# Paired numerators as two sets of 128 columns, a later share of one output projection, and a reordered last stretch

## The chip, the cores and the metric

The kernel runs on one core of one Trainium2 chip. The metric is the device time in microseconds (us) of one execution; smaller is better.

## What is computed

The input x is 2048 tokens of 512 numbers, all in float32. Two branches are mixed by a gate, token by token:

```
g = sigmoid((x * gate_w).sum(-1))
out = g * A(x) + (1 - g) * B(x)

A:  q, k, v = heads(x @ wqkv)                     # 32 heads of 16
    phi(p) = concat(softmax(p @ w_phi), softmax(-(p @ w_phi)))
    kv = sum over tokens of phi(k)^T v,  z = sum over tokens of phi(k)
    num = phi(q) kv,  den = phi(q) z + 1e-6
    A = concat over heads(num / den) @ wo
B:  per token and head the best of 16 keys in each of two halves: one of 256 experts
    B = sum over heads of gelu(x . u[expert]) * v[expert]
```

## The kernel before

The 2048 tokens are 16 tiles of 128. A first part (up to about 130 us) builds the weights and sums the keys and values of all tiles into `kvb`. The part that the change touches is the second: tile by tile it makes the output. Matrix products in full precision are made of three products of a high part (`xh`, `ch`, written by ScalarE, ACT) and a low part (`xl`, `cl`, the rest, written by VectorE, DVE, or GpSimd, POOL).

What one tile passes through, by the names in the trace:

- `s` (two halves of the scores against the keys), `pq` (the projected queries) and `pp` (the products with the experts' rows and the gate): matrix products, lines 55 to 57, into banks of a ring of four named "mm". DVE reads `s` in `best` (lines 736 and 737) and `pq` in `soft_in` (lines 123 to 129).
- The weighted feature map `d` of the queries. ACT splits it into two planes of 16-bit halves (`pl`, line 757), a DMA on SP's queue transposes them (`tp`, line 759), and ACT joins the halves again into `ptb` (`join`, two calls of `join_half`, line 768). The join of tile t writes the place t % 2 of `ptb`.
- The numerators `oT` = `kvb` times `ptb` (`mid_num`, line 777): 16 small matmuls of 64 rows by 32 columns of weights, 8 heads' worth in two tiles of PSUM. For a pair of tiles the same 16 matmuls take 256 columns, 128 of each tile. ACT turns `oT` into `xh` (`num_hi`, line 785), DVE into `xl` (`num_lo`, line 791).
- The experts' counts (`count`, lines 810 to 842, on DVE), multiplied by the activations into the coefficients `cf` (`coef`, line 846). They are transposed in one of two ways. The long way: ACT splits (`plc`, line 851), SP's queue transposes by DMA (`tpc`, line 853), ACT joins (`ctj`, line 858) and takes the high part (`ch`, line 862), POOL or DVE the low part (`cl`, line 879). The short way, `back_c`: TensorE transposes into `CT` (line 871), ACT takes `ch` (line 874), DVE `cl` (line 879).
- The output projection `po` (called `end` for the last tile): 18 matmuls of 512 columns, in this order: eight that read `xh` (line 891), four that read `xl` (line 891), and six that read `ch` and `cl` (line 898). `store` copies `po` to `ot` on ACT (line 929) and issues a DMA on SP's queue (line 930).

The order of the work on every engine is written out by hand; each engine takes its instructions in that order. The function `turned(a)` holds the order of one turn: it works at the front of tile a+1, in the middle of tile a, and at the back of tiles before it. `mid_num` is called for one tile at a time up to turn 5, then for a pair in the turns 7, 9, 11 and 13; the fifth pair (12 and 13) is in the last stretch. How many of the `po` matmuls are issued by the end of turn a, counted over all tiles, is `due(a)`: 15, 29 and 43 for the turns 2, 3 and 4. `back_some` issues what is due, at two places of a turn, and never past the end of a tile of 18 in one call; when a tile's 18 are out it calls `store`.

After turn 14 comes the last stretch, also written by hand, with a = 15, b = 14 and z = 13: it holds what is left of the tiles 10 to 15.

Of the kernel before, what the change touches and what calls it, by code (L numbers as in the profile page):

```python
# [20 lines left out]
P = 128  # L21
# [13 lines left out]
def mix_kernel(ctx, tc, xT, wqT, wkT, wv, wphi, wo, wq, kk, ug, ev, cst, out):  # L35
    nc = tc.nc
    pe, dve, act, pool, sp = nc.tensor, nc.vector, nc.scalar, nc.gpsimd, nc.sync
# [4 lines left out]
    def mm_bank(name):  # L42
        return psum.tile([P, 512], F32, tag="mm", bufs=4, name=name)

    def tr_bank(name):
        return psum.tile([P, 512], F32, tag="tr", bufs=3, name=name)
# [12 lines left out]
    kvb = per.tile([P, 8, 32], F32, name="kvb")  # L59
# [14 lines left out]
    def x_of(t):  # L74
        first = max(f for f in SEC if f <= t)
        return tuple(xt[i, first][:, t - first] for i in range(2))
# [253 lines left out]
    st8 = {t: {} for t in range(NT)}  # L330
# [146 lines left out]
    for t in range(5, NT - 1, 2):  # L477
        n = t + 1
# [13 lines left out]
        a = pks[t] = mm_bank(f"pk{t}")  # L492
        prod(a, tile_of(t, 0), b11, True)
        b = mm_bank(f"pu{t}")
# [89 lines left out]
    t = NT - 1  # L584
# [41 lines left out]
    def drain(t):  # L626
        while t in chains:
            step(t)
# [30 lines left out]
    def gelu_in(t):  # L659
        px, x2 = st8[t]["G"], st8[t]["x2"]  # L660
        pool.tensor_tensor(x2, x2, px, op=ALU.mult)

    def gelu_act(t):
        x2, gs = st8[t]["x2"], st8[t]["g"]
        act.activation(gs[:, 3:4], gs[:, 2:3], AF.Copy, scale=-0.5, bias=0.5)
        act.activation(x2, x2, AF.Tanh)
        act.activation(x2, x2, AF.Identity, bias=gs[:, 3:4], scale=gs[:, 3:4])

    def gelu_out(t):
        px, x2 = st8[t]["G"], st8[t]["x2"]  # L670
        pool.tensor_tensor(px, x2, px, op=ALU.mult)
# [33 lines left out]
    def soft_y(t, i):  # L705
        e = st8[t]
        dve.tensor_reduce(pair(e["st"][:, 224:288])[:, :, i], hs(e["w"], i), axis=AX.X, op=ALU.add)  # L707
# [45 lines left out]
    def planes(t, i):  # L753
        e = st8[t]
        e.setdefault("tp", [])
        pl = w3.tile([P, 2, 512], U16, tag="pl", name=f"pl{i}_{t}")
        act.copy(pl, e["ph"][:, halves[i]].bitcast(U16).rearrange("p (c j) -> p j c", j=2))  # L757
        tp = w3.tile([P, 8, P], U16, tag="tp", name=f"tp{i}_{t}")
        sp.dma_start_transpose(tp, pl.rearrange("p j c -> p (j c)"))
        e["tp"].append(tp)  # L760

    def join(t):
        for i in range(2):
            join_half(t, i)

    def join_half(t, i):
        p16 = ptb.rearrange("p g t n -> p (g t n)").bitcast(U16).rearrange("p (g t n j) -> p t j g n", j=2, n=P, t=2)
        act.copy(p16[:, t % 2, :, 4 * i:4 * i + 4, :], st8[t]["tp"][i].rearrange("p (j g) n -> p j g n", j=2))  # L768

    def mid_num(*ts):  # L770
        o = [tr_bank(f"oT{q}_{ts[0]}") for q in range(2)]
        u = slice(0, 2) if len(ts) > 1 else slice(ts[0] % 2, ts[0] % 2 + 1)
        n = 2 * P if len(ts) > 1 else P
        for g in range(8):
            for q in range(2):
                r0, c0 = 64 * q, 32 * (g % 4)
                pe.matmul(o[q][c0:c0 + 32, (g // 4) * n:(g // 4 + 1) * n], kvb[r0:r0 + 64, g, :],  # L777
                          ptb[r0:r0 + 64, g, u, :], start=(g < 4), stop=True, skip_group_check=True)
        for i, t in enumerate(ts):
            st8[t]["o"] = x_of(t) + ([m[:, :2 * n].rearrange("p (k t n) -> p t k n", k=2, n=P)[:, i] for m in o],)  # L780

    def num_hi(t):
        oh, ol, o = st8[t]["o"]
        for q in range(2):
            act.copy(oh[:, 2 * q:2 * q + 2], o[q])
# [58 lines left out]
    def coef(t):  # L844
        e = st8[t]
        (pool if t < NT - 1 else dve).tensor_tensor(e["C"], e["C"], e["G"], op=ALU.mult)  # L846

    def c_planes(t):
        e = st8[t]
        pl = w4.tile([P, 2, NX], U16, tag="plc", bufs=1, name=f"plc{t}")  # L850
        act.copy(pl, e["C"].bitcast(U16).rearrange("p (c j) -> p j c", j=2))
        e["tc"] = w4.tile([P, 4, P], U16, tag="tpc", bufs=1, name=f"tpc{t}")
        sp.dma_start_transpose(e["tc"], pl.rearrange("p j c -> p (j c)"))
# [13 lines left out]
    def back_c(t):  # L867
        e = st8[t]
        o = mm_bank(f"CT{t}")
        for j in range(2):  # L870
            pe.transpose(o[:, j * P:(j + 1) * P], e["C"][:, j * P:(j + 1) * P], ident)
        ch = w4.tile([P, 2 * P], F32R, tag="ch", name=f"ch{t}")
        cl = w4.tile([P, 2 * P], F32R, tag="cl", name=f"cl{t}")
        act.copy(ch, o[:, :2 * P])
        e["c"] = (ch, cl, o)

    def back_cl(t, eng=dve):
        ch, cl, o = st8[t]["c"]
        eng.tensor_tensor(cl, o[:, :2 * P], ch, op=ALU.subtract)
# [4 lines left out]
    def back_mm(t, cols=slice(0, D), bank=None):  # L884
        e = st8[t]
        oh, ol, _ = e["o"]
        po = bank
        mms = [(oh[:, k, :], w[k][:, cols]) for k in range(NK) for w in (woh, wol)]
        mms += [(ol[:, k, :], woh[k][:, cols]) for k in range(NK)]
        for i, (a, b) in enumerate(mms):  # L890
            pe.matmul(po, a, b, start=(i == 0), stop=False)  # L891
            yield
        ch, cl, _ = e["c"]
        js = (slice(0, P), slice(P, 2 * P))
        mms = [(ch[:, js[j]], w[:, j, cols]) for j in range(2) for w in (eh, el)]
        mms += [(cl[:, js[j]], eh[:, j, cols]) for j in range(2)]
        for i, (a, b) in enumerate(mms):
            pe.matmul(po, a, b, start=False, stop=(i == 5))  # L898
            yield
# [3 lines left out]
    def back(t, n=18):  # L903
        if t not in backs:
            split_ = t < NT - 5
            e = st8[t]
            e["po"] = psum.tile([P, 512], F32, tag="acc", name=f"po{t}") if split_ else mm_bank(f"po{t}")
            backs[t] = back_mm(t, bank=e["po"])
        for _ in range(n):
            next(backs[t])  # L910
# [1 line left out]
    ran = 0  # L912

    def due(a):
        return 14 * a - (13 if a < 7 else 14)

    def back_some(n):
        nonlocal ran
# [7 lines left out]
    def store(t):  # L926
        po = st8.pop(t)["po"]
        ot = w3.tile([P, D], F32, tag="ot", name=f"ot{t}")
        act.copy(ot, po)
        sp.dma_start(out[t * P:(t + 1) * P, :], ot)  # L930
# [65 lines left out]
    def turned(a):  # L996
# [7 lines left out]
        if a == 2:  # L1004
            mid_num(z)
            num_hi(z)
            gelu_pre(a)
# [6 lines left out]
        if 2 < a < 5:  # L1014
            back_some(due(a) - ran)
# [6 lines left out]
        if a < 5:  # L1022
            if a == 2:
                front_s(n, 1)
            else:
                mid_num(z)
                num_hi(z)
            if a == 3:
                front_s(n, 1)
            if masks:  # L1030
                mid_mask(*masks)
            if a > 3:
                front_s(n, 1)
            soft_exp(a)
        else:
            front_s(n, 1)
            soft_exp(a)
            if nums:
                mid_num(*nums)
            if parted is not None:  # L1040
                num_hi(parted)
            if masks:
                mid_mask(*masks)
            back_some(due(a) - ran)
# [12 lines left out]
        if a == NT - 2:  # L1057
            front_q(n)
        front_p(n, False)
        back_some(due(a) - ran)  # L1060
        best(n, 0)
        soft_y(a, 0)
# [13 lines left out]
    for a in range(NT - 1):  # L1076
        n, b, z = a + 1, a - 1, a - 2
# [4 lines left out]
        if a == 1:  # L1082
# [7 lines left out]
            ptb = spare_[:, :16 * P].rearrange("p (g t n) -> p g t n", t=2, n=P)  # L1090
# [48 lines left out]
    a, b, z = NT - 1, NT - 2, NT - 3  # L1139
# [18 lines left out]
    num_hi(z - 1)  # L1158
    back(z - 2, 6)
    num_hi(z)  # L1160
    join(b)
    store(z - 3)
    soft_y(a, 0)
    soft_y(a, 1)
    for _ in gate(a):
# [3 lines left out]
    coef(z - 1)  # L1169
    coef(z)  # L1170
    c_planes(z - 1)
    planes(a, 0)
    planes(a, 1)
    num_lo(z - 1)
# [10 lines left out]
    c_join(z - 1)  # L1185
    back_cl(z - 1, pool)
    back_c(z)
    store(z - 2)
    gelu_in(a)
    gelu_act(a)  # L1190
    gelu_out(a)
    back(z - 1, 6)
    back(b, 12)
    step(a, 4)
    back_cl(z)
    join(a)
    store(z - 1)
    back(z, 3)
    mid_num(a)
    num_hi(a)  # L1200
    back(z, 3)
    store(z)
    drain(a)
    num_lo(a)
# [1 line left out]
    coef(a)  # L1206
    end = mm_bank("end")
    ends = back_mm(a, bank=end)
    for _ in range(12):
        next(ends)  # L1210
    back_c(b)
    back_c(a)
    back_cl(b)
    back_cl(a)
    back(b, 6)
    store(b)
    for _ in range(6):
# [59 lines left out]
```

## Time and profile before

| | |
|---|---|
| median of 3 runs | 368.77 us (368.05 to 369.68) |
| the profiled execution | 368.4 us |
| its span, first to last instruction | 366.7 us |
| TensorE (PE) busy | 358.5 us, 98% |
| VectorE (DVE) busy | 318.4 us, 87% |
| ScalarE (ACT) busy | 256.7 us, 70% |
| GpSimd (POOL) busy | 207.5 us, 57% |

The profile was taken on one execution; 1.7 us of its 368.4 lie outside the span. "PEld" is TensorE's loading of weights, which runs beside its matmuls. A row of the timeline gives the start, the length, the engine, the line of the kernel, what is written from what, how many instructions are taken together, and in brackets how long the engine was idle before and what ended that. Matmuls overlap: the length of one is over the distance to the next. One of the small float32 matmuls shows as two rows. In the chain of work that ended last, each row is a start, a length and the work that the end waited for at that time.

### The profile page before, as it was taken

To read this page: it belongs to the slowest core of one execution; us is meant where nothing else is said; L and a number is where in the kernel's file an instruction comes from. 1 tells how busy PE (TensorE), PEld (TensorE's weight loads), DVE (VectorE), ACT (ScalarE), POOL (GpSimd) and SP (SyncE) were. 2 spreads that over 40 slices of the span, in tenths; PEclk is the share of its full clock that TensorE was granted. 3 is DMA by queue.
4 is the path that set the end of the run, shared out by engine and by line. 5 is a ranking of instruction groups with operands and counts; after the bars stand their busy time and mean duration, and the time that the engine had idled before them with its cause. 6 is when DMAs were issued, how large, how long until landed. Compare 5 with 4: busy or idle time off the path is not lost.

```text
span 366.7 us, 8308 instructions
## 1 busy us (share of the span) xinstructions
PE 358.5 (98%) x3244; PEld 280.1 (76%) x3244; DVE 318.4 (87%) x639; ACT 256.7 (70%) x455; POOL 207.5 (57%) x205
## 2 busy tenths in 40 slices
PE   8999999999999999999999999999999999999985
PEld 4766767776878878887788887887887887887764
DVE  4679999999878888999998897799879998899781
ACT  5586578876656765795696866866778886765871
POOL 1179989988928847445446546524724736527130
PEclk9999999999999999999999999999999999999999
DMA  7868898558773113144362244234343247234532
GB/s 267 332 241 273 273 259 246 156 179 300 240 212 100 62 30 69 35 86 67 79 116 64 67 86 88 74 86 84 62 98 90 55 104 103 73 88 100 66 93 86
DMA packets 75751, 47.54 MB, mean 130 GB/s; under 512 B 67265, under 2 KB 68161, under 8 KB 73409
## 3 DMA queue, kind: packets, MB, share of 16 engines
q1 hardware_dynamic: 74848, 46.15, 47.9%
q10 hardware_dynamic: 864, 0.87, 0.8%
q8 instruction: 25, 0.41, 0.5%
q14 instruction: 14, 0.11, 0.1%
HBM read 26.43 MB, written 4.19 MB: 84 GB/s over the span
## 4 chain that ended last, share of the span: by engine, by line
PE 75%; DVE 11%; ACT 4%; POOL 4%; DMA 3%; issue 2%; SPq 0%; POOLq 0%; ACTq 0%; DVEq 0%
PE po L891 8%; PE s L55 5%; PE s L57 5%; PE s L56 5%; PE pk L467 5%; PE po L898 4%; PE pu L467 4%; PE ws L300 4%; PE pq L57 3%; PE pq L56 3%; PE pq L55 3%; PE pe L467 2%; PE oT L777 2%; PE kvacc L291 2%; PE pv L467 2%
## 5 line engine op out<-in xcount | busy, mean ns | idle before, releaser
L728 POOL TENSOR_TENSOR d<-d,st 128x512 f32<-128x512 f32 x30 | 32.5, 1105 | 48.2 <-DVE st L721 47.0
L699 POOL TENSOR_TENSOR w<-d,zb 128x512 f32<-128x512 f32 x32 | 41.2, 1310 | 19.8 <-ACT d L693 19.8
L55 PE MATMUL s<-sh,xh 128*128 128x512 f32 x128 | 50.4, 394 | 0.0
L56 PE MATMUL s<-sl,xh 128*128 128x512 f32 x128 | 49.9, 389 | 0.0
L57 PE MATMUL s<-sh,xl 128*128 128x512 f32 x128 | 49.8, 389 | 0.0
L757 ACT COPY pl<-d 128x1024 uint16<-128x1024 uint16 x32 | 33.3, 1047 | 20.2 <-POOL d L728 20.1
L768 ACT COPY ptb<-tp 128x1024 uint16<-128x1024 uint16 x32 | 41.5, 1369 | 0.6 <-DMA tp<-pl 0.4
L284 POOL TENSOR_TENSOR d<-d,st 128x1024 f32<-128x1024 f32 x16 | 32.6, 2036 | 8.7 <-ACT d L275 6.5
L846 POOL TENSOR_TENSOR cf<-cf,px 128x256 f32<-128x256 f32 x15 | 11.1, 741 | 33.5 <-DVE cf L842 33.5
L55 PEld LDWEIGHTS s<-sh,xh 128*128 128x128 f32 x128 | 24.0, 188 | 5.3 <-issue 0.4
L57 PEld LDWEIGHTS s<-sh,xl 128*128 128x128 f32 x128 | 24.0, 188 | 5.0
L56 PEld LDWEIGHTS s<-sl,xh 128*128 128x128 f32 x128 | 24.0, 188 | 4.8
L55 PE MATMUL pq<-wah,xh 128*128 128x512 f32 x64 | 25.2, 393 | 0.0
L57 PE MATMUL pq<-wah,xl 128*128 128x512 f32 x64 | 24.9, 390 | 0.0
L56 PE MATMUL pq<-wal,xh 128*128 128x512 f32 x64 | 24.9, 389 | 0.0
L703 DVE TENSOR_REDUCE st<-d 128x32 f32<-128x512 f32 x32 | 20.5, 678 | 4.3 <-ACT d L693 4.1
L164 DVE TENSOR_TENSOR xl<-xr,xh 128x512 fp32r<-128x512 f32 (+2 forms) x17 | 21.7, 1292 | 1.7 <-ACT xh L160 1.6
L737 DVE TENSOR_TENSOR eq<-s,mx 128x512 bf16<-128x512 f32 x32 | 22.1, 691 | 1.1
L736 DVE TENSOR_REDUCE mx<-s 128x32 f32<-128x512 f32 x32 | 21.7, 680 | 0.2 <-PE s L57 0.2
L707 DVE TENSOR_REDUCE st<-w 128x32 f32<-128x512 f32 x32 | 20.5, 675 | 0.9 <-POOL w L699 0.9
L279 DVE TENSOR_REDUCE st<-d 128x64 f32<-128x1024 f32 x16 | 19.3, 1209 | 2.0 <-ACT d L275 1.9
L275 ACT ACTIVATE d<-d 128x1024 f32<-128x1024 f32 x16 | 17.0, 1066 | 4.1 <-DVE d L129 4.1
(271 smaller groups left out, 1086.2 us busy)
## 6 DMA issues: line engine op xcount, KB each, us to landing
wq<-wq SPq DMA_DIRECT2D x16, 1024.0 KB, 5.5
xr<-xT SPq DMA_DIRECT2D x15, 256.0 KB, 5.3
y<-ot SPq DMA_DIRECT2D x15, 256.0 KB, 2.0
rawk<-wkT SPq DMA_DIRECT2D x1, 1024.0 KB, 5.8
rawq<-wqT SPq DMA_DIRECT2D x1, 1024.0 KB, 6.3
rawu<-ug SPq DMA_DIRECT2D x2, 258.0 KB, 5.9
rawv<-wv ACTq DMA_DIRECT2D x2, 256.0 KB, 4.6
rawv<-wv SPq DMA_DIRECT2D x2, 256.0 KB, 5.3
```

Of the source, the lines that this page charges most:

```text
L55: pe.matmul(o, ah, bh, start=(first and i == 0), stop=False)
L56: pe.matmul(o, ah, bl, start=False, stop=False)
L57: pe.matmul(o, al, bh, start=False, stop=(last and i == n - 1))
L164: dve.tensor_tensor(l[:, ks], rawx[t][:, ks], h[:, ks], op=ALU.subtract)
L284: pool.tensor_tensor(g64(d), g64(d), b64(st[:, 128:192]), op=ALU.mult)
L467: pe.matmul(o, x_, w_, start=(first and i + j == 0), stop=(i == 1 and j == 2), skip_group_check=True)
L699: pool.tensor_tensor(hs(e["w"], i), hs(e["ph"], i), hs(zb, i), op=ALU.mult)
L728: eng.tensor_tensor(g64(d)[:, gs_], g64(d)[:, gs_], r[:, gs_].unsqueeze(2).to_broadcast([P, 32, F]), op=ALU.mult)
L737: dve.tensor_tensor(e["eq"][:, 512 * half:512 * half + 512].rearrange("p (h f) -> p h f", f=F), p3, mx.unsqueeze(2).to_broadcast([P, H, F] ...
L757: act.copy(pl, e["ph"][:, halves[i]].bitcast(U16).rearrange("p (c j) -> p j c", j=2))
L768: act.copy(p16[:, t % 2, :, 4 * i:4 * i + 4, :], st8[t]["tp"][i].rearrange("p (j g) n -> p j g n", j=2))
L891: pe.matmul(po, a, b, start=(i == 0), stop=False)
```

## The change

Four things are changed. (1) `mid_num` for a pair no longer gives each of the 16 weights 256 columns. It goes over the 16 weights with the 128 columns of the first tile, and then again with those of the second: 32 matmuls of 128 columns. The numerators of one tile now lie side by side in PSUM. (2) `due(3)` is 26 in place of 29. (3) In the last stretch the split `plc` of tile 12's coefficients stands between the two halves of the join of tile 14; the stores of the tiles 10, 11 and 12 are later. (4) The last two transposes `back_c` stand after ten of the last tile's matmuls in place of twelve.

```diff
     def mid_num(*ts):
         o = [tr_bank(f"oT{q}_{ts[0]}") for q in range(2)]
-        u = slice(0, 2) if len(ts) > 1 else slice(ts[0] % 2, ts[0] % 2 + 1)
-        n = 2 * P if len(ts) > 1 else P
-        for g in range(8):
-            for q in range(2):
-                r0, c0 = 64 * q, 32 * (g % 4)
-                pe.matmul(o[q][c0:c0 + 32, (g // 4) * n:(g // 4 + 1) * n], kvb[r0:r0 + 64, g, :],
-                          ptb[r0:r0 + 64, g, u, :], start=(g < 4), stop=True, skip_group_check=True)
         for i, t in enumerate(ts):
-            st8[t]["o"] = x_of(t) + ([m[:, :2 * n].rearrange("p (k t n) -> p t k n", k=2, n=P)[:, i] for m in o],)
+            for g in range(8):
+                for q in range(2):
+                    r0, c0 = 64 * q, 32 * (g % 4)
+                    pe.matmul(o[q][c0:c0 + 32, (2 * i + g // 4) * P:(2 * i + g // 4 + 1) * P], kvb[r0:r0 + 64, g, :],
+                              ptb[r0:r0 + 64, g, t % 2, :], start=(i == 0 and g < 4), stop=True, skip_group_check=True)
+            st8[t]["o"] = x_of(t) + ([m[:, 2 * i * P:2 * (i + 1) * P].rearrange("p (k n) -> p k n", n=P) for m in o],)
...
-        return 14 * a - (13 if a < 7 else 14)
+        return 26 if a == 3 else 14 * a - (13 if a < 7 else 14)
...
-    join(b)
-    store(z - 3)
+    join_half(b, 0)
...
     c_planes(z - 1)
+    join_half(b, 1)
     planes(a, 0)
...
-    store(z - 2)
+    store(z - 3)
     gelu_in(a)
     gelu_act(a)
+    store(z - 2)
...
     join(a)
-    store(z - 1)
     back(z, 3)
     mid_num(a)
     num_hi(a)
     back(z, 3)
+    store(z - 1)
     store(z)
...
-    for _ in range(12):
+    for _ in range(10):
         next(ends)
     back_c(b)
     back_c(a)
     back_cl(b)
     back_cl(a)
+    for _ in range(2):
+        next(ends)
     back(b, 6)
```

TensorE between turns 3 and 4, before (`po` is that of tile 1, `pq` that of tile 4):

```order
L891 MATMUL po_2414<-gl,xh_65 128x512
L891 MATMUL po_2414<-wb_77,xh_65 128x512 x2
L891 MATMUL po_2414<-t1h,xl_68 128x512 x2
L891 MATMUL po_2414<-gh,xl_68 128x512
L55 MATMUL pq_2475<-wah,xh_65 128x512
```

The same place in the change:

```order
L889 MATMUL po_2414<-gl,xh_65 128x512
L889 MATMUL po_2414<-wb_77,xh_65 128x512 x2
L55 MATMUL pq_2472<-wah,xh_65 128x512
L56 MATMUL pq_2472<-wal,xh_65 128x512
L57 MATMUL pq_2472<-wah,xl_68 128x512
```

Three matmuls that read `xl` have moved behind the twelve of `pq`.

ScalarE in the last stretch, before, from the join of tile 14 on (`ot_4369` is the store of tile 10, `plc` belongs to tile 12, `pl_15` to tile 15):

```order
L768 COPY ptb<-tp_14_4262 128x2x4x128
L768 COPY ptb<-tp_14_4266 128x2x4x128
L929 COPY ot_4369<-po_4229 128x512
L851 COPY plc_4386<-cf_4376 128x512
L757 COPY pl_15_4390<-d_4285 128x1024
L757 COPY pl_15_4394<-d_4285 128x1024
```

The same place in the change:

```order
L768 COPY ptb<-tp_14_4326 128x2x4x128
L849 COPY plc_4462<-cf_4452 128x512
L768 COPY ptb<-tp_14_4330 128x2x4x128
L757 COPY pl_15_4467<-d_4349 128x1024
L757 COPY pl_15_4471<-d_4349 128x1024
```

The split `plc` has moved ahead of half a join, and the store of tile 10 has left this place.

ScalarE further on, before, up to the join of tile 15 (`ot_4471` is the store of tile 11):

```order
L874 CAST ch_4468<-CT_4465 128x256
L929 COPY ot_4471<-po_4309 128x512
L665 ACTIVATE gs_4296<-gs_4296 128x1
L666 ACTIVATE x_4443<-x_4443 128x256
L667 ACTIVATE x_4443<-x_4443,gs_4296 128x256
L768 COPY ptb<-tp_15_4392 128x2x4x128
```

The same place in the change (`ot_4548` is the store of tile 10, `ot_4555` that of tile 11):

```order
L872 CAST ch_4545<-CT_4542 128x256
L927 COPY ot_4548<-po_4293 128x512
L665 ACTIVATE gs_4360<-gs_4360 128x1
L666 ACTIVATE x_4520<-x_4520 128x256
L667 ACTIVATE x_4520<-x_4520,gs_4360 128x256
L927 COPY ot_4555<-po_4373 128x512
L768 COPY ptb<-tp_15_4469 128x2x4x128
```

The store of tile 10 stands where that of tile 11 stood, and the store of tile 11 directly ahead of the join of tile 15.

## The prediction

> **What bounds the kernel now.** First the page: its first lines give the span and the busy shares.
>
> ```profile
> span 366.7 us, 8308 instructions
> PE 358.5 (98%) x3244; PEld 280.1 (76%) x3244; DVE 318.4 (87%) x639; ACT 256.7 (70%) x455; POOL 207.5 (57%) x205
> ```
>
> TensorE is nearly full, so time is won only by making its work shorter or by taking away one of its few waits. The second view is therefore the list of TensorE's waits over the whole span; these three rows lie in the part that the change touches.
>
> ```profile
> PE po L898 <- ACT ch L862: 1.9, 1, 1.9
> ...
> PE po L891 <- DVE xl L791: 0.3, 1, 0.3
> PE po L898 <- ACT ch L874: 0.2, 1, 0.2
> ```
>
> Each happened once: 1.9, 0.3 and 0.2 us. These 2.4 us are nearly all that the change can win; the rest must come from what TensorE costs to stop and start. The third view is the chain that ended last, read in the last stretch, where the engine that sets the end is no longer TensorE alone.
>
> ```profile
> 340.61 2.47 ACT ptb L768 x2
> 343.08 0.45 ACT ot L929
> 343.53 0.52 ACT plc L851
> ...
> 344.07 4.30 DMA tpc<-plc
> ...
> 348.39 0.77 ACT ctj L858
> ...
> 349.67 0.74 POOL cl L879
> 350.41 1.19 POOL x L661
> ...
> 351.62 0.43 ACT x L666
> ...
> 352.58 2.59 ACT ptb L768 x2
> ...
> 355.21 0.45 PE oT L777 x16
> ...
> 356.56 2.77 PE end L891 x12
> 359.32 0.23 PE CT L871 x2
> ...
> 359.58 0.38 ACT ch L874
> ...
> 360.00 1.66 PE po L898 x6
> ```
>
> The reader is to see that from 340.6 to 355.2 the path runs over ACT, a transposing DMA and POOL, and comes back to TensorE only when the second half of the join of tile 15 is done. What is taken off ACT's row there counts, and what is put on it counts too.
>
> **The pairs as two sets.** A pair's visit now, and a single tile's visit, with the instruction that follows each; then the loads of weights in the single visit.
>
> ```profile
> 338.22 1.09 PE L777 MATMUL oT<-ptb,kvb 64*32 64x256 f32 x32
> 339.25 0.56 PE L800 MATMUL mk<-wm,et 128*128 128x16 bf16 x16
> ...
> 344.85 0.67 PE L777 MATMUL oT<-ptb,kvb 64*32 64x128 f32 x32
> 345.45 0.73 PE L891 MATMUL po<-t1h,xl 128*128 128x512 f32 x2
> ```
>
> ```profile
> 344.85 0.40 PEld L777 LDWEIGHTS oT<-ptb,kvb 64*32 64x32 f32 x32 [0.35 <-issue]
> ```
>
> From first start to the next work a pair takes 1.03 us and a single tile 0.60. The number of matmuls is the same, 16; only the columns double. So 128 columns of all 16 weights cost 0.43, and entering and leaving costs 0.17. Two sets in one visit are 0.17 + 2 × 0.43 = 1.03: no change. The low end is a few hundredths below that; the high end is two whole visits, 1.20, or +0.17 a pair and +0.85 for five. I take zero, since a single visit already reloads its weights at this pace (32 loads in 0.40 of its 0.67). A sentence by itself: the Trainium skill, TensorEngine Tiling, section Performance Considerations (Instruction Overhead), gives each matmul about 60 cycles of overhead; at the 2.4 GHz of its page TensorE: Matmul & The Clock Gate that is an estimate of 25 ns, 0.4 us for 16 more matmuls and 2.0 us for five pairs, which would turn the sum below into a loss of 0.5 us. The row speaks against it: 32 rows in 0.67 us is 21 ns a row with everything in it.
>
> The split does not let ACT begin earlier: in the order with its waits, the conversions `xh` of the pair's first tile carry a wait on TensorE and those of the second carry none, so the first already wait for the last matmul. That is the same as before. ACT and DVE read the same number of columns.
>
> **Three matmuls later in turn 3.** This is where TensorE waited for `xl` of tile 1:
>
> ```profile
> 177.79 0.63 PE L891 MATMUL po<-wb,xh 128*128 128x512 f32 x2
> 178.71 0.74 PE L891 MATMUL po<-t1h,xl 128*128 128x512 f32 x2 [0.30 <-DVE xl L791]
> 179.29 0.39 PE L891 MATMUL po<-gh,xl 128*128 128x512 f32 x1
> ```
>
> Two matmuls take 0.46 when they run without a stop (179.29 − 178.71 = 0.58 here, after the stop). From 177.79 the next should start at 178.25; it started at 178.71. The stop costs 0.46 and the slow start 0.12: 0.58. The change puts the 12 matmuls of `pq` there, whose bank has long been read, and the three come 2.7 us later, when `xl` is done. TensorE is 0.58 ahead from turn 4 on. What is late next? DVE is busy for 13.48 of these 14.00 us (the third engine of the row) and waits for no matmul in them, so it does not come along:
>
> ```profile
> 184.00:198.00 14.00, 14.00 (x97) 11.47 (x97) 13.48 (x33) 10.44 (x20) 6.66 (x8) 1.00 0.48 85
> ```
>
> The nearest thing for which TensorE would then wait is the bank of the second half of `s` of tile 5, which DVE's `best` reads last here, and which the second half of tile 6 needs:
>
> ```profile
> 197.43 0.69 DVE L737 TENSOR_TENSOR eq<-s,mx 128x512 bf16<-128x512 f32 x1
> ```
>
> ```profile
> 198.59 0.39 PE L55 MATMUL s<-sh,xh 128*128 128x512 f32 x1
> ```
>
> DVE is done at 198.12, TensorE would be there at 198.01: a new wait of about 0.16 with a signal's time, and again a slow start of 0.12. I take 0.58 − 0.28 = **0.30** as the gain, between 0 (if it is all given back) and 0.58. From turn 6 on DVE itself waits for `pq`, as here, so the shift is handed on to it:
>
> ```profile
> 237.09 0.69 DVE L123 TENSOR_REDUCE st<-pq 128x32 f32<-128x512 f32 x1 [1.24 <-PE pq L57]
> ```
>
> **The last stretch, up to the 1.9 us wait.** I keep the times of before. `plc` now starts after one half join: 340.61 + 1.24 = 341.85 in place of 343.53. Its input is there: both coefficients of the pair are ready when POOL ends at 341.35.
>
> ```profile
> 339.91 1.44 POOL L846 TENSOR_TENSOR cf<-cf,px 128x256 f32<-128x256 f32 x2 [1.79 <-DVE cf L842]
> ```
>
> The DMA then starts at 342.39 and, at its 4.30, lands at 346.69; the view of this tile gives its landing over all its issues:
>
> ```profile
> DMA to landing us min/median/max: 2.3/2.3/4.3
> ```
>
> So 4.30 is the worst of thirteen, and on SP's queue the store of tile 10 no longer stands ahead of it. ACT's own row, without that store, is 0.45 earlier, and then no longer stops for the DMA:
>
> ```profile
> 348.39 0.76 ACT L858 COPY ctj<-tpc 128x512 uint16<-128x512 uint16 x1 [0.91 <-DMA tpc<-plc]
> ```
>
> ```profile
> 349.64 0.50 PE L898 MATMUL po<-eh,ch 128*128 128x512 f32 x1 [1.86 <-ACT ch L862]
> ```
>
> `ctj` starts at 348.39 − 0.45 − 0.91 = 347.03, after the landing. Everything behind it is 1.36 earlier, the first TensorE matmul on `ch` too: 349.64 becomes 348.28. Of the 1.9 us wait about 0.5 is left, since ACT's row is now the bound. Splitting the join of tile 14 makes its second half 0.07 later (0.52 for `plc`, less 0.45 for the store); TensorE reads it only at 344.85, so that costs nothing.
>
> **From there to the join of tile 15.** POOL's `cl` and `x`, and ACT's two steps behind them, come 1.36 earlier. But the store of tile 11, which ACT did while it waited for POOL, now stands directly ahead of the join: +0.45. The join ends 0.91 earlier. TensorE must wait for it:
>
> ```profile
> 354.64 1.03 PE L777 MATMUL oT<-ptb,kvb 64*32 64x128 f32 x32
> ```
>
> TensorE comes to this visit 5.00 after 349.64 now, hence at 353.28 in the change, is through its first half at 353.73, and the join's second half is there at 355.21 − 0.91 = 354.30. ACT sets the time: **0.91**. Bounds: 1.36 if the store were hidden again; 0.46 if the landing or the join of tile 15 were late by half a microsecond. The store of tile 12, now behind the conversions of tile 15, stands where ACT next waits for the last matmuls of tile 13, and costs nothing.
>
> **The last transposes.**
>
> ```profile
> 359.16 0.60 PE L871 MATMUL CT<-cs,cf 128*128 128x128 f32 x4
> ```
>
> ```profile
> 356.83 0.45 DVE L846 TENSOR_TENSOR cf<-cf,px 128x256 f32<-128x256 f32 x1
> ```
>
> After the four transposes (first row) TensorE waits until 360.00. Two matmuls of 0.23 now fill that: they hide the 0.24 of idle time and some of the transposes' draining, less a slow start. I take **0.30**, between 0.2 and 0.4. The transposes come earlier by 0.91 + 0.46, at 357.8; their last input now ends at 357.28, and DVE's part comes earlier too.
>
> **The sum.** 0 − 0.30 − 0.91 − 0.30 = −1.51 us. Against the profiled execution (span 366.7, 368.4 with what lies around it) that is 366.9. The profiled execution lies 0.4 below the median of the runs, 368.77, so the median becomes 367.3, or −0.41%. About 0.5% (1.84 us) is what a measurement of this kernel can tell from no change.
>
> **The rivals.** *More is hidden* (0.29). Either the wait at 198 does not come, because DVE is a little earlier (+0.28), or ACT's store of tile 11 falls into idle time because a shorter DMA and the earlier TensorE leave some (+0.45). One of them gives −1.8 to −2.0, both −2.2: 366.6 to 367.0, take 366.8. For it: the margin at 198 is 0.1 us. Against: ACT has no idle time left ahead of the join in my account.
>
> *Two sets cost two visits* (0.15). +0.17 a pair, 0.85 in five, four of them in stretches where TensorE never waits, the fifth ahead of ACT's row: −0.7, 368.1. For it: nothing shows 32 such matmuls in one visit. Against: the 0.17 is the change of shape at both ends of a visit.
>
> *The weights are not hidden* (0.06), the slower side. The second set loads the same places of the array that the first is still using. If each load waited for its matmul, a visit would be 0.17 + 0.86 + 2 × 0.40 = 1.83, +0.80 a pair, +4.0 in five: 368.77 − 1.5 + 4.0 = 371.3. It decides from +0.30 a pair on (no gain) and is past 0.5% slower from +0.67. The Trainium skill, TensorE: Matmul & The Clock Gate, Part 3, says that loads overlap matmuls in flight only for another group of rows, and there are only two groups here. Against it: in the single visit weights are changed in the same places halfway, in 0.67 in all.
>
> **How the numbers follow.** The forecast has 0.50, −1.2 to −1.8. Its faster end and the first rival give faster by over 0.5%: 0.05 + 0.29 = 0.34. The rest of the forecast and the second rival lie within 0.5%: 0.45 + 0.15 = 0.60. Slower is the third: 0.06. The range leaves out the third rival and the outer ends of the first two: 366.3 to 368.6.
>
> **What would show it.** In the changed profile: pair visits of 64 rows, 1.05 to 1.12 long, next work 1.03 after the start. No wait for `xl` near 178, and one of 0.1 to 0.3 for `eq` near 198. No wait of ACT for `tpc` in the last stretch; TensorE's wait for `ch` (line 860) 0.4 to 0.7 in place of 1.9; its wait for the join of tile 15 about half a microsecond; no wait for `ch` of line 872 at the end. I am wrong if the pair's visit is over 1.2, if TensorE's wait for `ch` stays above 1 us, or if the gain of turn 3 is gone by the last stretch.

## The result and the profile after

The change runs in 366.94 us (median of 4 runs, 366.46 to 367.27), the kernel before beside it in 369.22 (4 runs, 368.05 to 369.68): a ratio of 0.9942 [0.9914, 0.9971]. Measured a second time, it was 367.15 (8 runs) against 368.86 (15 runs): 0.9933 [0.9905, 0.9961]. So it is faster, by 0.6 to 0.7%: both intervals lie below 1, with their near ends at 0.3% and 0.4%. The forecast was 367.3 and −0.41%: the time lies in the range, the gain is a little larger than foretold. The profiled execution took 367.09 us, with this page:

```profile
span 365.3 us, 8628 instructions
PE 358.8 (98%) x3404; PEld 282.2 (77%) x3404; DVE 318.5 (87%) x639; ACT 256.7 (70%) x455; POOL 206.6 (57%) x205
```

TensorE's share is the same 98%; it has 160 matmul rows and 160 loads more (five pairs of 32), and its busy time is 0.3 longer, not shorter. The gain is in its waits. The list of them, which leaves out stops of about a tenth of a microsecond, now has these:

```profile
PE warm L357 <- POOL tab L339: 1.1, 1, 1.1
PE pv L56 <- DVE wbr L50: 0.6, 1, 0.6
PE pv L55 <- ACT wbr L49: 0.4, 1, 0.4
PE po L896 <- ACT ch L860: 0.3, 1, 0.3
PE oT L776 <- ACT ptb L768: 0.2, 1, 0.2
```

The wait of 1.9 us for `ch` has shrunk to 0.3, those for `xl` and for the last `ch` are gone, and a wait of 0.2 for the join of tile 15 (`ptb`) is there, which the prediction had, only longer. A wait for `eq` near 198, which it also had, is not there. The chain that ended last, in the last stretch:

```profile
343.69 1.85 ACT pl L757 x2
...
347.08 0.69 ACT ctj L856
...
347.80 0.41 ACT ch L860
...
350.67 0.60 ACT x L667
351.28 0.47 ACT ot L927
351.75 2.48 ACT ptb L768 x2
...
354.27 0.45 PE oT L776 x16
```

The transposing DMA, 4.30 us of the chain before, has left it: the path stays on ACT's row up to `ch`, and comes back to it behind POOL's `cl` and `x`. The store of tile 11 (`ot`, 0.47) stands on it now. From 354.27 up to the last copies nothing but TensorE is on the path.

**A measure that can tell tenths.** Full times of single executions swing by one to three microseconds, because the first 150 us do: the first numerators of tile 0 start at 150.95 in the execution before and at 151.40 after, and at 151.45 and 154.04 in the two profiled executions of one kernel (`best`, below). From there on the two profiled executions agree to 0.03, in both kernels that were profiled twice. So the runs below are read by two distances inside the profiled execution. D goes from the start of tile 0's numerators to the start of VectorE's last copy, T from the start of the last pair's numerators to the same copy. The rows of before, then of after, from the timelines of TensorE and VectorE:

```profile
150.95 0.67 PE L777 MATMUL oT<-ptb,kvb 64*32 64x128 f32 x32
```

```profile
363.08 0.42 DVE L1222 COPY ot_end<-end 128x256 f32<-128x256 f32 x1 [2.34 <-PE end L898]
```

```profile
151.40 0.67 PE L776 MATMUL oT<-ptb,kvb 64*32 64x128 f32 x32
...
338.29 1.16 PE L776 MATMUL oT<-ptb,kvb 64*32 64x128 f32 x64
```

```profile
361.68 0.42 DVE L1223 COPY ot_end<-end 128x256 f32<-128x256 f32 x1 [2.33 <-PE end L896]
```

D is 212.13 before and 210.28 after; T is 363.08 − 338.22 = 24.86 before and 23.39 after. So 1.85 us were won, 1.47 of them in the last stretch and 0.38 before it. The second profile of the change gives 210.26 and 23.39; that of `best` 208.99 and 22.63, beside 208.96 and 22.60.

| | D | T | full time of the profiled execution |
|---|---|---|---|
| before | 212.13 | 24.86 | 368.4 |
| the change | 210.28 | 23.39 | 367.09 |
| due_only | 211.18 | 24.83 | 368.82 |
| pairs_one_set | 209.99 | 23.31 | 366.44 |
| sets_of_64 | 212.07 | 23.65 | 369.32 |
| plc_late | 211.36 | 24.47 | 367.53 |
| store10_early | 210.77 | 23.88 | 368.6 |
| store11_hidden | 209.82 | 22.94 | 367.78 |
| end_12 | 210.70 | 23.83 | 367.4 |
| best | 208.96 | 22.60 | 365.73 |
| best_2 | 208.37 | 22.02 | 364.75 |

### The profile page after: what moved, and what is told of

It is laid out like the page before. It is cut to its first block, busy times and chain, and to the rows that moved or that the text cites. A ratio compares the mean times of both kernels' runs of the same rounds, so it can differ in the third digit from the quotient of the medians.

```text
span 365.3 us, 8628 instructions
## 1 busy us (share of the span) xinstructions
PE 358.8 (98%) x3404; PEld 282.2 (77%) x3404; DVE 318.5 (87%) x639; ACT 256.7 (70%) x455; POOL 206.6 (57%) x205
## 4 chain that ended last, share of the span: by engine, by line
PE 86%; ACT 5%; POOL 3%; DMA 2%; DVE 2%; issue 1%; SPq 0%; POOLq 0%; ACTq 0%; DVEq 0%
PE po L889 9%; PE s L55 7%; PE s L56 7%; PE s L57 7%; PE pk L467 5%; PE po L896 5%; PE pu L467 4%; PE ws L300 4%; PE pq L55 4%; PE pq L56 4%; PE pq L57 4%; PE oT L776 2%; PE kvacc L291 2%; PE pp L55 2%; PE pp L56 2%; PE pp L57 2%
## 5 line engine op out<-in xcount | busy, mean ns | idle before, releaser
L927 ACT COPY ot<-po 128x512 f32<-128x512 f32 x15 | 8.7, 589 | 16.3 <-PE po L896 14.8
```

## The experiments

**Only the later share of turn 3 (due_only).** The kernel before, with one line of the change:

```diff
-        return 14 * a - (13 if a < 7 else 14)
+        return 26 if a == 3 else 14 * a - (13 if a < 7 else 14)
```

> The kernel before with due(3) = 26 alone. All distances are taken in one execution from the first numerator matmul of tile 0 (turn 2) to the start of the last copy on VectorE: 212.13 us before, 210.28 in the change. Theory: the stop of TensorE for the low part of tile 1 goes with its slow start, nothing takes its place, and the rest of the loop moves along: 211.5 us, no wait of TensorE near 198 us, and the 1.9 us wait for ch in the last stretch stays, since ScalarE's row moves along too. First rival, as the prediction had it: TensorE then waits for the bank that VectorE's best reads last, 211.8. Second rival: what is won is given back at a later wait, 212.1.

The visit of turn 4 starts 35.69 after tile 0's in the kernel before and 35.10 here: 0.59 won, and in turn 5 (50.45 and 49.86) it is still 0.59. D is 0.95 shorter: 0.59, and 0.33 more that were lost in turn 8 before and not here. The edit alone does not decide these 0.33: the change has it too and lost most of them (last section). T is 24.83 against 24.86, so nothing is given back at the end. TensorE's two waits for `ch`, 1.9 and 0.2, stay, and that for `xl` is gone.

**Pairs as one set in the changed kernel (pairs_one_set).** The change with the numerators of before:

```diff
+        for g in range(8):
+            for q in range(2):
...
+                pe.matmul(o[q][c0:c0 + 32, (g // 4) * n:(g // 4 + 1) * n], kvb[r0:r0 + 64, g, :],
+                          ptb[r0:r0 + 64, g, u, :], start=(g < 4), stop=True, skip_group_check=True)
         for i, t in enumerate(ts):
-            for g in range(8):
-                for q in range(2):
...
-                    pe.matmul(o[q][c0:c0 + 32, (2 * i + g // 4) * P:(2 * i + g // 4 + 1) * P], kvb[r0:r0 + 64, g, :],
-                              ptb[r0:r0 + 64, g, t % 2, :], start=(i == 0 and g < 4), stop=True, skip_group_check=True)
```

> The change with the pair's numerators again as one set of 256 columns; all else as in the change. Theory: the two sets cost 0.06 us in each of five visits, so the distance from the first numerator matmul of tile 0 to the last copy goes from 210.28 to about 209.95 us, and the next work stands 1.03 us after a visit's start in place of 1.09. Rival: the two sets gain something elsewhere (a conversion that starts earlier, reads that lie side by side), then the distance is 210.3 or more.

D is 0.29 shorter than the change's, T 0.08: about 0.07 for each of four pairs. The first pair, in turn 7, shows nothing in D: both kernels start turn 9's visit 104.02 after tile 0's, since the stop in turn 8 is 0.06 longer here (last section). The visits of the last pair show what one costs; first what follows the change's (which starts at 338.29, above), then this run:

```profile
339.38 0.56 PE L798 MATMUL mk<-wm,et 128*128 128x16 bf16 x16
```

```profile
337.81 1.09 PE L777 MATMUL oT<-ptb,kvb 64*32 64x256 f32 x32
338.84 0.31 PE L800 MATMUL mk<-wm,et 128*128 128x16 bf16 x6
```

So two sets take 1.09 to the next work (339.38 − 338.29) and one set 1.03 (338.84 − 337.81). This part of the change loses.

**Pairs as four sets of 64 columns (sets_of_64).** What sets the pace of many small matmuls:

```diff
+            for h in range(2 if len(ts) > 1 else 1):
+                w_ = P // 2 if len(ts) > 1 else P
...
+                        s0 = (2 * i + g // 4) * P + h * w_
+                        pe.matmul(o[q][c0:c0 + 32, s0:s0 + w_], kvb[r0:r0 + 64, g, :],
+                                  ptb[r0:r0 + 64, g, t % 2, h * w_:(h + 1) * w_],
+                                  start=(i == 0 and h == 0 and g < 4), stop=True, skip_group_check=True)
```

> The change with a pair's numerators as four sets of 64 columns (64 matmuls a visit; the same columns and the same result). Theory: the first 16 matmuls of a visit stand ready when it begins, and behind them each further matmul takes at least some 27 ns to be issued whatever its columns are; then the next work stands about 0.17 + 0.21 + 48 x 0.027 = 1.7 us after the start of a visit in place of 1.09, and the distance from the first numerators to the last copy is about 213.2 us. Rival: the columns set the pace and each border between two sets costs 0.06; then the next work stands 1.2 us after the start and the distance is 210.9.

The four visits in the turns took 1.41, 1.59, 1.48 and 1.41 to the next work, and T rose by 0.26: 4 visits and T together are the 1.79 that D is longer than the change's.

```profile
228.62 1.48 PE L779 MATMUL oT<-ptb,kvb 64*32 64x64 f32 x128
230.03 0.56 PE L802 MATMUL mk<-wm,et 128*128 128x16 bf16 x16
```

1.2 at a constant 0.06 for each border between two sets is out: three borders cost 0.38 and more. 1.7 (27 ns a matmul) was too high. Read row by row, the first 33 rows of the visit start within 0.27 us, eight in 56 ns, then there is a stop of about 0.07, and from there the rows come singly, 8 to 9 ns apart at the least (17 ns a matmul) and often 17 ns. So beyond the first 33 rows the pace is set by the issue of matmuls, not by columns. The visits of 1.48 and 1.59 have one more stop each, of 0.05 and 0.09; what for, the rows don't say.

In the change's own visit, with 128 columns, the rows do not fall behind: eight start every 0.109 us from the second eight to the last, the 33rd row among them (0.461 after the first). Only the loads of weights stop, for 0.08 behind the 33rd, and from there the rows of an eight come singly. The last row of the visit so starts 0.10 after the first of its eight, in place of 0.05 with one set: this is 0.05 of the 0.06.

**The split of tile 12's coefficients after the whole join (plc_late).**

```diff
+    join_half(b, 1)
     c_planes(z - 1)
-    join_half(b, 1)
     planes(a, 0)
```

> The change with the split plc of tile 12 behind both halves of the join of tile 14; the store of tile 10 stays where the change put it. Theory A (the store was what hurt: 0.45 us in ScalarE's row, and its 256 KB on the DMA queue ahead of the transposing DMA, which then took 4.3 us instead of 2.3): the DMA starts at about 343.7 and lands by 347, when ScalarE needs it, and the distance stays at 210.3 us within 0.1. Theory B (the early place of the split is what helps; the transposes of tile 15 right behind it make the landing 4.3 again): ScalarE waits about 1 us for the landing, and the distance is 211.0 to 211.3.

D and T are both 1.08 longer than the change's. The store of tile 10 is still away from here, yet the transposing DMA takes 4.4 again and ACT stands still for it, and TensorE behind ACT; ACT's timeline, then TensorE's waits:

```profile
347.51 0.76 ACT L856 COPY ctj<-tpc 128x512 uint16<-128x512 uint16 x1 [1.00 <-DMA tpc<-plc]
```

```profile
PE po L896 <- ACT ch L860: 1.4, 1, 1.4
```

So a store ahead in SP's queue is not needed for the long landing. Theory B took the transposes of tile 15, close behind in that queue, for the cause. Its time came (211.36), and these rows fit it: first this run, SP's queue and then the landing in the view of the tile `tpc`; then the same two of the change:

```profile
343.11 1.19 SPq L851 DMA_TRANSPOSE tpc<-plc  x1
344.39 2.55 SPq L759 DMA_TRANSPOSE tp<-pl  x1
```

```profile
DMA to landing us min/median/max: 4.4/4.4/4.4
```

```profile
342.45 1.19 SPq L851 DMA_TRANSPOSE tpc<-plc  x1
344.62 3.45 SPq L759 DMA_TRANSPOSE tp<-pl  x2
```

```profile
DMA to landing us min/median/max: 2.3/2.3/2.3
```

1.28 behind, the landing is 4.4; 2.17 behind, it is 2.3. It was 2.3 too in store10_early, end_12 and best_2, where the split stands between the half joins. But two earlier issues in the change's own profile speak against theory B. In the first the transposes of `eq` follow 1.28 behind, and the landing is 2.3; in the second they follow 3.25 behind, and it is 4.4:

```profile
263.08 1.19 SPq L851 DMA_TRANSPOSE tpc<-plc  x1
264.36 1.26 SPq L743 DMA_TRANSPOSE et<-eq  x1
```

```profile
287.58 1.19 SPq L851 DMA_TRANSPOSE tpc<-plc  x1
290.83 1.23 SPq L743 DMA_TRANSPOSE et<-eq  x1
```

What goes with the long landing is another transfer: a packet of 16 KB that the view of the DMA queues calls "instruction", by its name a load of the program's own instructions. From the issue to 2.4 us behind it this view has one in plc_late (below) and in the kernel before, and none in the change, where it starts only at 345.26, behind the landing. The last section has the count over all profiles.

```profile
q8 instruction: 1, 0.02, 4.0%
```

So the early place of `plc` wins by its earlier issue: with 4.4 the DMA would have landed at 346.85 in the change, still ahead of `ctj` at 346.97.

**The store of tile 10 back on ACT ahead of tile 15's planes (store10_early).**

```diff
     c_planes(z - 1)
     join_half(b, 1)
+    store(z - 3)
     planes(a, 0)
...
     back_c(z)
-    store(z - 3)
     gelu_in(a)
```

> The change with the store of tile 10 back at its old place on ScalarE, between the join of tile 14 and the planes of tile 15; the split plc keeps its new place between the two halves. The measure is the last stretch: from the start of the last pair's numerators on TensorE to the start of VectorE's last copy, 24.86 us before and 23.39 in the change. Theory: the store's 0.46 us lie on ScalarE's row, which sets the time up to the join of tile 15; its transfer does not matter, since the transposing DMA is then already ahead of it: 23.85, and TensorE's wait for ch grows from 0.35 to 0.8 us. Rival: the store's 256 KB slow the transposes again (landing 4.3 us and more for tile 12, late for tile 15) and the last stretch takes 24.3 or more.

T is 0.49 longer, the length of the store on ACT's row (344.60 to 345.07 here), the landing of `tpc` stays 2.3, and TensorE's wait grows by as much:

```profile
344.60 0.63 ACT L927 COPY ot<-po 128x512 f32<-128x512 f32 x1
345.07 1.10 ACT L757 COPY pl<-d 128x1024 uint16<-128x1024 uint16 x1
```

```profile
PE po L896 <- ACT ch L860: 0.8, 1, 0.8
```

So of the move of the store only its time on ACT counts.

**The store of tile 11 where ACT waits (store11_hidden).**

```diff
     store(z - 3)
+    store(z - 2)
     gelu_in(a)
     gelu_act(a)
-    store(z - 2)
     gelu_out(a)
```

> The change with the store of tile 11 right behind that of tile 10, in the time in which ScalarE waits for GpSimd's x, in place of directly ahead of the join of tile 15. Theory: the join is done 0.46 us earlier, TensorE comes to it at its own pace, its 0.20 us wait and the slow start go: the last stretch takes 23.1 in place of 23.39 us. Rival: the join was not what TensorE waited for (its transposes land late), then it stays at 23.4.

T is 22.94, 0.45 shorter: the store had cost that much ahead of the join. TensorE no longer stops between the two halves of the last numerators: here they are one row of 0.67, in the change, below it, two rows with a wait.

```profile
354.82 0.67 PE L776 MATMUL oT<-ptb,kvb 64*32 64x128 f32 x32
```

```profile
353.62 0.45 PE L776 MATMUL oT<-ptb,kvb 64*32 64x128 f32 x16
354.27 0.45 PE L776 MATMUL oT<-ptb,kvb 64*32 64x128 f32 x16 [0.20 <-ACT ptb L768]
```

The full time of this execution, 367.78, hides the gain: its first numerators started later, at 152.62. That is why D and T are used.

**The last transposes after twelve matmuls again (end_12).**

```diff
-    for _ in range(10):
+    for _ in range(12):
         next(ends)
...
-    for _ in range(2):
-        next(ends)
     back(b, 6)
```

> The change with the last two transposes behind all twelve matmuls of the last tile's projection, as before. Theory: two matmuls no longer cover the way from the transposes over ScalarE's ch back to TensorE, and the last stretch takes 23.85 in place of 23.39 us, with TensorE idle for about 0.24 us ahead of the matmuls on ch. Rival: the prediction's 0.30 was right and the rest of the gain there came from elsewhere: 23.69.

T is 23.83, 0.44 longer, and the wait of 0.24 is back behind the transposes:

```profile
358.07 0.60 PE L869 MATMUL CT<-cs,cf 128*128 128x128 f32 x4
358.92 0.50 PE L896 MATMUL po<-eh,ch 128*128 128x512 f32 x1 [0.24 <-ACT ch L872]
```

**The parts that win, without those that lose (best, best_timed).** One set for the pairs, the store of tile 11 behind the join of tile 15, and the coefficients of tile 12 joined ahead of tile 15's activations:

```diff
     mid_num(b)
-    gelu_rest(a)
     num_hi(b)
+    c_join(z - 1)
+    gelu_rest(a)
...
     num_lo(b)
-    c_join(z - 1)
...
     gelu_act(a)
-    store(z - 2)
...
     join(a)
+    store(z - 2)
     back(z, 3)
```

> The change with three edits: a pair's numerators again as one set of 256 columns; the conversions of tile 14's numerators and the join of tile 12's coefficients ahead of the three steps on px and x; the store of tile 11 behind the join of tile 15. Theory: ScalarE's row no longer sets the time anywhere in the last stretch, and TensorE's two waits there (0.35 for ch, 0.20 for the join) go with their slow starts: the last stretch takes 22.5 to 22.7 us (23.39 in the change), and from the first numerators to the last copy 209.2 to 209.4 (210.28 in the change). Rival: VectorE's counts for the tiles 14 and 15 become the bound, and TensorE waits ahead of the last transposes: 23.0 us or more.

T is 22.60, 0.79 shorter than the change's. D is 1.32 shorter: 0.79, the pairs of the turns 9, 11 and 13 at 0.07, and 0.33 up to turn 9, where the stop of turn 8 and the first pair's 0.06 are gone. A new wait stands there: the transposes into `CT` need a bank that ACT's activation step (line 647, now later) still reads.

```profile
347.66 0.41 PE L871 MATMUL CT<-cs,cf 128*128 128x128 f32 x2 [0.52 <-ACT x L647]
```

> The kernel of best again, timed. Theory (the distances inside one execution add up to the time): 1.3 us below the change if VectorE's stop in turn 8 falls as in its first execution, 1.0 if not; so 0.6% to 0.9% below the kernel before, 0.991 +- 0.002. Rival: the first 150 us swing so much that no difference from the change can be told.

366.22 (8 runs) against 368.86: a ratio of 0.992 [0.9891, 0.9949]. The change's own second measurement stood beside it:

> The change itself, timed again beside the next two. All theories: a ratio of about 0.994 to the kernel before, within the interval of the first measurement; last stretch 23.39 us.

367.15 (8 runs): 0.9933 [0.9905, 0.9961]. The two intervals overlap; by the medians `best` is 0.9 faster than the change.

**The activations ahead of them again (best_2).** ACT's activations of tile 15 go first, so that the bank of `CT` is free early, and four steps of tile 15's count on VectorE go ahead of tile 14's `xl`. Against `best`:

```diff
     mid_num(b)
-    num_hi(b)
-    c_join(z - 1)
     gelu_rest(a)
+    c_join(z - 1)
+    num_hi(b)
     back(z - 1, 4)
     back(z, 4)
+    step(a, 4)
     num_lo(b)
...
     back(b, 12)
-    step(a, 4)
     back_cl(z)
```

> As best, but the three steps on px and x come first again, then the join of tile 12's coefficients, then the conversions of tile 14; VectorE does four steps of the count ahead of the low part of tile 14. In best TensorE waited 0.5 us for its transposes into CT, whose bank ScalarE's step on x still read. Theory: that wait goes with its slow start and nothing takes its place: the last stretch takes 22.0 us (22.60 in best). Rival: ScalarE's ch is now late by as much (a wait of 0.2 to 0.5 us for ch), 22.3 to 22.6.

365.14 (6 runs) against 368.86: 0.9882 [0.9851, 0.9914], the fastest of all. It beats the change too: its slowest run, 366.58, is below the fastest of the change measured beside it, 366.61, and the medians are 2.0 us apart. T is 22.02, 0.58 below `best`, of which the wait of 0.52 is the most. The list of TensorE's waits has only two left, both in the first part (1.1 for `tab`, 0.2 for `wbr`), and the chain in the last stretch is TensorE's alone, from the last pair up to the last copies; here through the two places where the change waits, `ch` and the join of tile 15:

```profile
346.74 0.22 PE CT L871 x2
346.96 1.49 PE po L898 x6
...
351.87 0.60 PE oT L777 x32
```

## Why the prediction was right or wrong, point by point

**Right: what bounds the kernel.** TensorE is full, and what a change wins are its waits and its stops. The three waits held most of the gain, and ACT's row, not TensorE, set the time of the last stretch up to the join of tile 15. The sum was −1.51 for one execution; measured by D it is −1.85.

**Turn 3: 0.30 foretold, 0.59 won. The step that failed** is "the nearest thing for which TensorE would then wait is the bank of the second half of `s` of tile 5, which DVE's `best` reads last here, and which the second half of tile 6 needs". The stop of 0.58 went, as worked out. The wait of 0.28 that was to take its place did not come. TensorE starts the second half of tile 6 in its even pace while VectorE still reads the second half of tile 5. The overlap is plainest in store11_hidden, which has the same instructions up to the last stretch: TensorE starts at 199.67, VectorE reads until 199.11 + 0.69 = 199.80.

```profile
199.67 0.39 PE L55 MATMUL s<-sh,xh 128*128 128x512 f32 x1
```

```profile
199.11 0.69 DVE L737 TENSOR_TENSOR eq<-s,mx 128x512 bf16<-128x512 f32 x1
```

The load of this matmul's weights, which carries the wait for VectorE, starts earlier still, at 199.45. In the change itself the matmul starts at 198.45 and the read ends at 198.54. So that half does not wait for that read, and cannot be in that bank if a bank is reused only behind its last read; no view shows the bank. The prediction took the ring of four to be filled in fixed turn and did not look up which earlier reader the matmul's wait stands for. This was the rival "more is hidden" in its first form, though for another reason than the one it gave (VectorE a little earlier).

**The pairs: zero foretold, 0.06 a visit measured, 0.29 in D.** A mis-sized term, inside its bounds of a few hundredths below zero and 0.17 above. The error is in "a single visit already reloads its weights at this pace": the single visit has 32 rows and 32 loads, and the loads stop behind the 33rd, which only the longer visit has. The rivals with two whole visits (+0.17 a pair) and with weights that are not hidden (+0.80) are out. The estimate by 25 ns a matmul (the Trainium skill, TensorEngine Tiling, 0.4 us a visit) is also out, by 0.06; the prediction's own argument against it was weak, since it set 21 ns a row against a figure for a matmul, which has two rows (42 ns). Where the loads stop is near another figure of the Trainium skill: TensorE: Matmul & The Clock Gate, in the table at its head, gives TensorE's queue 64 entries, and 32 matmul rows with their 32 loads are 64. That the queue is the cause was not tried by itself.

**The last stretch up to the wait for `ch`: 1.36 foretold, 1.52 won.** From the pair's start to the first matmul on `ch` it is 349.64 − 338.22 = 11.42 before, and this row less 338.29, 9.96, after, with the pair's 0.06 in it:

```profile
348.25 0.50 PE L896 MATMUL po<-eh,ch 128*128 128x512 f32 x1 [0.35 <-ACT ch L860]
```

The step held: ACT's row is 0.45 shorter without the store (store10_early, 0.49) and does not stop for the DMA (plc_late, 1.08). Of the rest of 0.16, 0.12 is that `ctj` now starts before the step ahead of it has ended (346.46 + 0.63 = 347.09), where the stop had kept them apart:

```profile
346.46 0.63 ACT L783 CAST xh<-oT 128x256 fp32r<-128x256 f32 x2
346.97 0.79 ACT L856 COPY ctj<-tpc 128x512 uint16<-128x512 uint16 x1
```

The account had kept the landing at 4.30, so it did not need the one that came, 2.3, which it owes to where a load of instructions fell (plc_late); its aside on the store of tile 10 ahead in SP's queue is not borne out, since plc_late has 4.4 without that store. What is left of TensorE's wait is 0.35, where about 0.5 was foretold.

**The join of tile 15: 0.91 foretold, 1.01 measured.** The second half of tile 15's numerators starts 16.99 after the pair before (355.21 − 338.22) and 15.98 after (354.27 − 338.29). The store of tile 11 gave back 0.45, as priced; store11_hidden takes it away and wins exactly that. TensorE's wait there is 0.20, where about half a microsecond was foretold, since TensorE comes later to it: 353.62 − 348.25 = 5.37 after its first matmul on `ch`, not 5.00. It stops twice on the way, too shortly for the list of waits: ahead of the matmuls on POOL's `cl` (349.37, 0.31 after the one before in place of 0.23) and right behind them (349.98, 0.61 later in place of 0.46); with the slow starts this is 0.36 of the 0.37.

**The last transposes: 0.30 foretold, 0.44 measured** (end_12). A mis-sized term. From the first of the four transposes to the first matmul on `ch` it is 0.85 without the two matmuls (end_12, 358.92 − 358.07) and 0.90 with them in between (the change, 358.67 − 357.77). So of their 0.45 all but 0.05 is hidden: they fill the wait of 0.24 and most of the time in which TensorE came to a stop and started again, which the prediction had taken off the gain.

**The sum.** Turn 3 −0.59; the pairs of the turns 9, 11 and 13 +0.21 (that of turn 7 is hidden in the stop of turn 8); the last stretch up to the join −1.01, with its own pair in it, and behind the join −0.46: together the −1.85. The gain is made of the right parts. But that the sum comes near is in part luck: two errors of nearly 0.3, on turn 3 and on the pairs, have opposite signs and cancel, and what is left is the three tenths by which the last stretch was undersized (0.16 up to the join without the pair, 0.14 to 0.16 on the transposes).

## What to carry to other kernels

Where one engine is full, a change is a list of its stops, and each stop costs its wait plus a slow restart: fill it with work whose inputs have long been ready. Before foretelling that a wait is replaced by another on the same buffer, look up which reader the next user's wait really stands for. An item that is moved off a critical row has to go to a place where its engine waits anyway: the store of tile 10 won 0.49 by leaving such a row, that of tile 11 lost 0.45 by being put on it.

## What the runs showed of the hardware that was not expected

**A race of two engines for 1 us, in turn 8.** Near 240 us VectorE's operation on `ptb` and GpSimd's product `w` start within a tenth of a microsecond of each other. In the kernel before VectorE's took 1.55; in due_only it took 0.42, and GpSimd's pair 3.02 instead of 2.73. VectorE and GpSimd of before, then of due_only:

```profile
240.41 1.55 DVE L828 TENSOR_SCALAR ptb<-ptb 128x512 uint32<-128x512 uint32 x1
```

```profile
240.39 2.73 POOL L699 TENSOR_TENSOR w<-d,zb 128x512 f32<-128x512 f32 x2 [2.39 <-ACT d L693]
```

```profile
241.18 0.42 DVE L828 TENSOR_SCALAR ptb<-ptb 128x512 uint32<-128x512 uint32 x1
```

```profile
241.16 3.02 POOL L699 TENSOR_TENSOR w<-d,zb 128x512 f32<-128x512 f32 x2 [2.37 <-ACT d L693]
```

Behind the long one, `cl` is about a microsecond later and TensorE stops for it: in the kernel before its first matmul on `cl` starts 0.45 after the one before it (243.46 − 243.01) in place of 0.23, and the next work 0.57 behind that in place of 0.45. This costs 0.33 of D there and in pairs_one_set, and 0.27 in the change, where TensorE comes 0.06 later to it. It was short in due_only and in the profiles of best, best_timed and best_2, and long in all others, pairs_one_set among them, which has the same instructions as best up to the last stretch. So the instructions up to there do not decide it. The two kernels that were profiled twice came out the same both times (the change long, best short), so it stays open whether it falls anew in each execution. What decides it can't be read from the rows: in both kernels GpSimd's starts 0.02 ahead of VectorE's. The Trainium skill, GPSIMD Engine Reference, section 1 (Specifications), says that GpSimd shares its paths to the on-chip memory with VectorE, and that they collide when VectorE's instruction is in its two-port mode or has two inputs there; a stretch from 0.42 to 1.55 fits that, and the size is this trace's. That it is this collision was not tried by itself.

**A transposing DMA lands late when a load of instructions falls into it.** The DMA of `tpc` was issued 169 times in the thirteen profiles, and for 168 the landing can be read. In 125 of them no instruction packet was in flight from the issue to 2.45 us behind it: they landed after 2.29 to 2.38 us, 33 of them with the next transposes less than 1.5 behind. In 16 such a packet began 0.97 to 2.44 behind the issue: 15 of them landed after 3.9 to 4.4, and the other, whose packet began at 2.38, had landed at 2.33. With a packet that began between 0.14 ahead of the issue and 0.81 behind it, the landing took 2.5 to 3.1. No run moved such a packet by itself, so the two go together in every case seen, but how one holds up the other was not tried.

**Small matmuls run at two paces in one visit.** In sets_of_64 eight rows of 64 columns start in 56 ns up to the 33rd row; after that 8 to 9 ns a row is the least that was seen. In the change, with 128 columns a row, eight rows take 0.109 us on both sides of it.
